# One shift term of the VectorE exponentials computed by GpSimd in four paired pieces, with the scheduler's constants retuned

## The chip, the cores and the metric

The kernel runs on one core of one Trainium2 chip. The metric is the device time of one execution in microseconds. A core has five engines that matter here: PE (TensorE, matrix multiply), DVE (VectorE), ACT (ScalarE), POOL (GpSimd) and SP (which issues DMAs). Each executes its own instructions in order; semaphores connect them. Times of a kernel agree within about 0.3% on a quiet chip. The granted TensorE clock differed between chips and runs in this study (0.97 to 1.00), and before's time with it (1559 to 1581 us), so it is given wherever it matters.

## The reference, cut to what matters

Four residual blocks in a row: A, B, A, B, on x of 2048 tokens x 512 features. A is attention with 32 query heads of size 16 and one shared key/value head; B is linear attention.

```python
def _A_ref(x, wq, wk, wv, wo):
    ...
    scores = jnp.einsum("bhqd,bkd->bhqk", q, k) * (Dh ** -0.5)
    p = _softmax(scores, axis=-1)
    o = jnp.einsum("bhqk,bkd->bhqd", p, v)
    ...
x = x + _A_ref(_layernorm(x, axis=-1), A_wq, A_wk, A_wv, A_wo)
x = x + _B_ref(_layernorm(x, axis=-1), B_wqkv, B_wo)
# ... and both once more
```

Block A dominates. Each of the two A layers has 2048 x 2048 x 32 scores. The kernel cuts them into 2048 blocks of 128 keys x 512 queries a layer, 4096 in all; each has to be computed (PE), exponentiated (ACT or DVE) and multiplied with the values (PE).

## The kernel before

The kernel contains a list scheduler. While the program is built, it simulates the five engines with fixed durations and a table of priorities and thresholds (the constants at its top), decides the order of instructions on each engine, and emits them in that order. Nothing is decided on the chip. In particular, which blocks go to ACT and which to DVE is settled at build time.

A block goes one of two ways.

ACT takes sets of three or two blocks from PSUM (banks 0 to 2, 3 to 4) in one exp instruction. Each block then needs one PV matmul.

```python
oe = add(AC, tac(m * 512), lambda e: e.activation(PTA[:, hp.idx, 0:m * 512], bank(SETS[s][0], m * 512), ACTF.Exp, scale=SCALE),
         deps=[o] + prevp, uses=[h, hp], rel=[h], prio=1.0, name="exp")
```

DVE takes single blocks from PSUM banks 5 and 6 and approximates exp by writing a scaled score as an integer whose bits are read as bf16 ("P1", one PSUM read a block). The approximation is refined by three more terms: copies of the tile with 32, 64 or 96 added to the integer ("xo", the shifts, 2048 columns for a batch of four blocks). PE adds the four terms up, with a scaled copy of the values for each. So a block on DVE needs four PV matmuls, and bank, DVE and PE in turn.

```python
o = add(PE, PASS, lambda e: self.smm(e, [p], db), ..., prio=0.01, name="sD", ...)          # score of one block
o = add(DV, tdv(512), lambda e: e.tensor_scalar(out=PTD[:, hp.idx, i * 512:(i + 1) * 512], in0=bank(db),
        scalar1=SCALE * LOG2E * 128.0, scalar2=TOFF, op0=ALU.mult, op1=ALU.add), ..., prio=PP1, name="P1")
...
def dpass(self, c):                                # a batch is full: its terms and PV matmuls
    ...
    for r in range(NTERM):                         # NTERM = 4
        dep, src = c["p1"], hp
        if r:
            dep, src = self.shift(c, m, r, done)
        for i, p in enumerate(c["pos"]):
            pv = self.add_pv(p, lambda src=src, i=i: PTD[:, src.idx, i * 512:(i + 1) * 512].bitcast(BF16), src, dep[0 if r else i], r, 1)
            ...
def shift(self, c, m, r, done):
    ...
        return e.tensor_scalar(out=PTD[:, ht.idx, 0:512 * m], in0=PTD[:, hp.idx, 0:512 * m], scalar1=float(SHIFT[r]), op0=ALU.add, **kw)
    o = add((DV, PO) if POOLX else DV, ..., prio=PX, cb=done, name="xo", port=True)
```

The softmax here doesn't subtract the row's maximum and nothing guards it: scores larger than these inputs give would overflow.

## Time and profile before

1562.74 us, median of 3 runs (1561.04 to 1565.96).

| before | value | view |
|---|---|---|
| PE, ACT, DVE, POOL busy | 96%, 95%, 94%, 11% | the page |
| ACT and DVE busy, 100-700 us | 97%, 96% | windows |
| blocks on ACT / on DVE | 3013 / 1083 | groups (PV and P1 counts) |
| 2048-wide shifts on DVE | 810, 0.67 us each | groups |

From the page: span, busy time by engine, granted PE clock in 40 slices, and the shares of the chain of waits that ended last.

```profile
span 1562.1 us, 41630 instructions
...
PE 1504.2 (96%) x18426; PEld 493.7 (32%) x18426; DVE 1467.4 (94%) x2631; ACT 1480.0 (95%) x1451; POOL 166.5 (11%) x225
...
PEclk9999999999999999999999999999999999999999
...
PE 58%; DVE 21%; ACT 20%; issue 1%; DMA 0%; POOL 0%; SPq 0%
...
```

PE, ACT and DVE are all nearly full; GpSimd is nearly idle (11%). The groups of DVE, ACT, POOL and PE that matter (columns: line, engine, operation, output<-input, shapes, count | busy us, mean ns | idle us just before them and what ended it):

```profile
...
L963 DVE TENSOR_SCALAR PTD<-ps_all 128x512 uint16<-128x512 f32 x1083 | 724.4, 682 | 42.8 <-PE ps_all L749 38.3
L1010 DVE TENSOR_SCALAR PTD<-PTD 128x2048 uint16<-128x2048 uint16 x810 | 546.3, 688 | 1.6
...
```

```profile
...
L906 ACT ACTIVATE PTA<-ps_all 128x1536 bf16<-128x1536 f32 (+1 forms) x1199 | 1386.6, 1282 | 40.6 <-PE ps_all L749 36.5
...
```

```profile
...
L1133 POOL TENSOR_TENSOR pqT<-e_buf 128x512 bf16<-128x512 f32 x28 | 38.4, 1376 | 10.2 <-DVE e_buf L1129 9.5
L1131 POOL TENSOR_SCALAR e_buf<-e_buf 128x512 f32<-128x512 f32 x56 | 37.9, 678 | 408.5 <-ACT e_buf L1122 408.4
...
```

```profile
...
L786 PE MATMUL ps_all<-PTD,Vaug 128*32 128x512 bf16 x4332 | 610.1, 386 | 13.3 <-DVE Eo L798 9.6 <-DVE PTD L1010 3.0
...
```

DVE waits little for its P1s (42.8 us), ACT little for its exps (40.6 us). GpSimd and the shifts disturb each other, as the timelines of DVE and POOL for the same moment show (columns: start us, us, instruction):

```profile
...
458.54 1.77 DVE L1010 TENSOR_SCALAR PTD<-PTD 128x2048 uint16<-128x2048 uint16 x1
460.23 0.24 DVE L811 RECIPROCAL rden<-ps_all 128x16 f32<-128x16 f32 x1
...
```

```profile
...
458.49 1.27 POOL L1133 TENSOR_TENSOR pk_tok<-e_buf 128x512 bf16<-128x512 f32 x1
```

The shift starts 0.05 us after GpSimd's add, and takes 1.77 us instead of 0.68. It ends 0.55 us after the add.

### The profile page before, as it was taken

What the parts mean: (1) busy time and instruction counts of PE and PEld (TensorE: products, weight loads), DVE (VectorE), ACT (ScalarE), POOL (GpSimd) and SP (SyncE); (2) the same over time, 40 slices, a digit from 0 to 9 for tenths busy, and PEclk for the clock granted to TensorE, in tenths of its full rate; (3) what the DMA queues carried; (4) which work ended last, traced back from release to release, by engine and by line L of the source; (5) the groups of instructions that cost most, each with busy time, mean ns of one, the idle gap of its engine ahead of it and who ended that gap; (6) DMA issues with size and microseconds to landing.
All of it is one profiled execution on the core that took longest, in us unless ns stands there. A gap on an engine that the chain in (4) does not pass through costs nothing.

```text
span 1562.1 us, 41630 instructions
## 1 busy us (share of the span) xinstructions
PE 1504.2 (96%) x18426; PEld 493.7 (32%) x18426; DVE 1467.4 (94%) x2631; ACT 1480.0 (95%) x1451; POOL 166.5 (11%) x225
## 2 busy tenths in 40 slices
PE   6999999999999999999899999999999999999998
PEld 4222222223323223332453222322223323223234
DVE  5999998999998999999799999999999999999987
ACT  6999999999999999999699999999999999999996
POOL 4000001002013001100330000000002112012011
PEclk9999999999999999999999999999999999999999
DMA  4000000000000000000000000000000000000001
GB/s 138 1 5 8 5 8 8 5 3 6 5 17 7 5 5 12 12 5 8 7 4 2 4 12 5 8 5 5 5 5 5 8 16 5 5 13 14 1 12 57
DMA packets 46181, 17.93 MB, mean 11 GB/s; under 512 B 39856, under 2 KB 45488, under 8 KB 46000
## 3 DMA queue, kind: packets, MB, share of 16 engines
q1 hardware_dynamic: 46000, 15.27, 4.1%
q8 instruction: 144, 2.36, 0.6%
q14 instruction: 37, 0.30, 0.1%
HBM read 5.28 MB, written 2.10 MB: 5 GB/s over the span
## 4 chain that ended last, share of the span: by engine, by line
PE 58%; DVE 21%; ACT 20%; issue 1%; DMA 0%; POOL 0%; SPq 0%
PE ps_all L786 23%; PE ps_all L749 23%; ACT PTA L906 18%; PE ps_all L498 10%; DVE PTD L963 10%; DVE PTD L1010 6%; PE ps_all L807 2%; DVE Eo L798 1%; ACT e_buf L1122 0%; DVE pqT L1252 0%; DVE x_sb L1114 0%; DVE stats L558 0%; PE ps_all L589 0%; ACT e_buf L1250 0%; DVE e_buf L1129 0%
## 5 line engine op out<-in xcount | busy, mean ns | idle before, releaser
L906 ACT ACTIVATE PTA<-ps_all 128x1536 bf16<-128x1536 f32 (+1 forms) x1199 | 1386.6, 1282 | 40.6 <-PE ps_all L749 36.5
L963 DVE TENSOR_SCALAR PTD<-ps_all 128x512 uint16<-128x512 f32 x1083 | 724.4, 682 | 42.8 <-PE ps_all L749 38.3
L749 PE MATMUL ps_all<-QT,Kr 32*128 32x512 bf16 x4154 | 679.1, 384 | 17.8 <-ACT PTA L906 12.8
L786 PE MATMUL ps_all<-PTD,Vaug 128*32 128x512 bf16 x4332 | 610.1, 386 | 13.3 <-DVE Eo L798 9.6
L1010 DVE TENSOR_SCALAR PTD<-PTD 128x2048 uint16<-128x2048 uint16 x816 | 547.9, 686 | 1.6
L786 PE MATMUL ps_all<-PTA,Vaug 128*32 128x512 bf16 x3013 | 532.8, 387 | 0.1
L749 PEld LDWEIGHTS ps_all<-QT,Kr 32*128 32x128 bf16 x4154 | 162.2, 91 | 502.6 <-ACT PTA L906 228.3
L786 PEld LDWEIGHTS ps_all<-PTD,Vaug 128*32 128x32 bf16 x4332 | 150.7, 94 | 218.1 <-issue 140.7
L786 PEld LDWEIGHTS ps_all<-PTA,Vaug 128*32 128x32 bf16 x3013 | 131.4, 94 | 187.5 <-issue 157.3
L566 POOL TENSOR_TENSOR rstd<-veps,mhalf 128x1 f32<-128x1 f32 x30 | 19.6, 654 | 875.5 <-DVE veps L564 875.5
L1131 POOL TENSOR_SCALAR e_buf<-e_buf 128x512 f32<-128x512 f32 x56 | 37.9, 678 | 408.5 <-ACT e_buf L1122 408.4
L498 PE MATMUL ps_all<-wqkv_sb,xnT 128*32 128x512 bf16 x1024 | 76.5, 388 | 0.6 <-DMA xnT<-xn_buf 0.4
L1122 ACT ACTIVATE e_buf<-ps_all 128x512 f32<-128x512 f32 x64 | 40.8, 641 | 12.6 <-PE ps_all L498 6.3
L498 PE MATMUL ps_all<-xnT,wq_sb 128*32 128x128 bf16 (+1 forms) x896 | 41.0, 293 | 4.1 <-issue 4.1
L558 DVE BATCH_NORM_STATS2 stats<-x_sb 128x6 f32<-128x512 bf16 x64 | 43.0, 678 | 0.8 <-DMA x_sb<-in_A_x_dram 0.7
L798 DVE COPY Eo<-ps_all 128x512 f32<-128x512 f32 x62 | 42.3, 682 | 1.0 <-PE ps_all L786 0.6
L1129 DVE TENSOR_SCALAR e_buf<-ps_all 128x512 f32<-128x512 f32 x56 | 38.1, 683 | 5.3 <-ACT e_buf L1122 5.0
L807 PE MATMUL ps_all<-identf,Eo 128*128 128x128 f32 x256 | 42.5, 289 | 0.2 <-DVE v_tok L1148 0.2
L498 PE MATMUL ps_all<-wo_sb,OT 128*32 128x512 bf16 x512 | 42.5, 382 | 0.0
L1133 POOL TENSOR_TENSOR pqT<-e_buf 128x512 bf16<-128x512 f32 x28 | 38.4, 1376 | 10.2 <-DVE e_buf L1129 9.5
L1133 POOL TENSOR_TENSOR pk_tok<-e_buf 128x512 bf16<-128x512 f32 x28 | 37.8, 1348 | 11.6 <-DVE e_buf L1129 8.7
L498 PE MATMUL ps_all<-xnT,wqkv_sb 128*32 128x128 bf16 (+1 forms) x896 | 37.4, 289 | 0.0
(90 smaller groups left out, 660.4 us busy)
## 6 DMA issues: line engine op xcount, KB each, us to landing
out_dram<-x_sb SPq DMA_DIRECT2D x16, 128.0 KB, 1.8
OT<-Osb SPq DMA_TRANSPOSE x120, 2.4
xnT<-xn_buf SPq DMA_TRANSPOSE x120, 2.4
wqkv_sb<-in_B_wqkv_dram SPq DMA_DIRECT2D x1, 1536.0 KB, 13.2
x_sb<-in_A_x_dram SPq DMA_DIRECT2D x3, 256.0 KB, 3.4
x_sb<-in_A_x_dram SPq DMA_DIRECT2D x1, 768.0 KB, 8.3
wq_sb<-in_A_wq_dram SPq DMA_DIRECT2D x1, 512.0 KB, 6.6
x_sb<-in_A_x_dram SPq DMA_DIRECT2D x1, 512.0 KB, 9.3
```

The costliest lines, as they stand in the source:

```text
L498: i = e.matmul(out[32 * c:32 * c + 32], lhsT=lhsT[:, 32 * c:32 * c + 32], rhs=rhs, start=start, stop=stop, skip_group_check=True)
L558: add(DV, tdv(512), lambda e: e.bn_stats(stats[:, t, 0:6], x_sb[:, t, :]), reads=[("x", t)], writes=[("st", t)], prio=prio, name="bn")
L749: x = e.matmul(bank(b0 + k), lhsT=Kr[r, m, kt * P:(kt + 1) * P], rhs=QT[r, self.units[u][0] % 2, gs, q0:q0 + n], start=True, stop=True)
L786: return e.matmul(ps[32 * c:32 * c + 32, 7 * 512:8 * 512], lhsT=Vaug[:, kt, r, :], rhs=src() if callable(src) else src, start=opened[0], s ...
L798: return (e.copy if oe.eng == AC else e.tensor_copy)(Eo[:, he.idx, :], bank(7))
L807: i = e.transpose(bank(ht.idx, P, qs * P), Eo[:, he.idx, qs * P:(qs + 1) * P], identf[:])
L906: oe = add(AC, tac(m * 512), lambda e: e.activation(PTA[:, hp.idx, 0:m * 512], bank(SETS[s][0], m * 512), ACTF.Exp, scale=SCALE), deps=[o] ...
L963: o = add(DV, tdv(512), lambda e: e.tensor_scalar(out=PTD[:, hp.idx, i * 512:(i + 1) * 512], in0=bank(db), scalar1=SCALE * LOG2E * 128.0, ...
L1010: return e.tensor_scalar(out=PTD[:, ht.idx, 0:512 * m], in0=PTD[:, hp.idx, 0:512 * m], scalar1=float(SHIFT[r]), op0=ALU.add, **kw)
L1122: o1 = add(AC, tac(512), lambda e: e.activation(e_buf[:, he.idx, :], bank(h.idx), ACTF.Exp), deps=[o], uses=[h], acq=[he] if fast else [he ...
L1129: o2 = add(DV, tdv(512), lambda e: e.tensor_scalar(out=e_buf[:, hr.idx, :], in0=bank(h.idx), scalar1=0.0, scalar2=1e-6, op0=ALU.max, op1=A ...
L1133: add(PO, PHS, lambda e: e.tensor_tensor(out=dst, in0=sh(e_buf[:, hr.idx, :]), in1=sh(e_buf[:, he.idx, :]), op=ALU.add), deps=[o2, o3], us ...
```

## The change

The intent: DVE is full and GpSimd idle, so GpSimd takes one of the three shifts of each full batch. A shift runs in a fast DVE mode that excludes GpSimd from SBUF, so the term is cut in four 512-wide pieces and each is tied to a DVE instruction that doesn't use the shared port: the scheduler starts a piece when DVE is in an instruction with at least PXM (0.55 us) left, and the piece then waits for the DVE instruction before that one. A piece that has waited PXA (4 us) may start in any DVE instruction that leaves the port free. Eleven older constants were retuned with it, most of all PX from 2.241 to 0.523 (shifts now come before P1s). The normalisation of odd tiles at a layer's start moved from GpSimd to DVE (PX1 = 0).

```diff
-HOLD = 0.75
+HOLD = 0.836
-PX = 2.241
+PX = 0.523
-PX1 = 1
-BK = 1.383
+PX1 = 0
+BK = 2.611
+NPX = 6
+PXP = 1.839
+PXM = 0.55
+PXA = 4.0
 ... (LEAD2, AF, EVP, PQP, PTR, BKX, PQL, PZ likewise)
@@ _try
+            if e == PO and o.pair and self.tfree[DV] - self.now < o.pair and self.now - o.rt < PXA - 1e-6:
+                self.at(o.rt + PXA, None)
+                continue
@@ _start
+        if e == PO and o.pair and len(self.order[DV]) > 1:
+            o.deps = o.deps + [self.order[DV][-2]]
@@ dpass
+                split = r == NTERM - 1 and m == 4 and self.npx < NPX and bool(p_ptd.free)
+                if split:
+                    dep, src = self.pieces(c, m, r, done)
+                elif r:
-                if r:
                     dep, src = self.shift(c, m, r, done)
@@ pieces (new; buffer bookkeeping cut)
+            for i in range(m):
+                def f(e, i=i):
+                    return e.tensor_scalar(out=PTD[:, ht.idx, i * 512:(i + 1) * 512], in0=PTD[:, hp.idx, i * 512:(i + 1) * 512], scalar1=float(SHIFT[r]), scalar2=1.0,
+                                           op0=ALU.add, op1=ALU.mult)
+                r_.append(add(PO, PXO[0] + 512 * PXO[1], f, deps=[c["p1"][i]] + prev, uses=[hp, ht], prio=PXP, cb=cb, name="xp", pair=PXM))
```

More of the change, by code (lines that the diff above doesn't have):

```diff
@@ L21 @@
 LX = 0.338
-HOLD = 0.75
+HOLD = 0.836
 LEAD = 16
-LEAD2 = 11
+LEAD2 = 14
 NT0 = 3
@@ L31 @@
 MF = 0.758
-AF = 2.752
+AF = 2.905
 PCONT = 0.992
-PX = 2.241
+PX = 0.523
 PP1 = 1.0
-EVP = 1.348
+EVP = 1.5
 EVX = 1.016
-PQP = 3.49
+PQP = 3.044
 PB = 1.6
@@ L41 @@
 PKV = 4.5
-PTR = 1.576
+PTR = 1.57
 PQF = 2
@@ L47 @@
 KC = 2
-PX1 = 1
-BK = 1.383
-BKX = 0.515
+PX1 = 0
+BK = 2.611
+BKX = 0.376
 BKR = 0.5
@@ L53 @@
 YD = 2
-PQL = 4.303
+PQL = 3.988
+NPX = 6
+PXP = 1.839
+PXM = 0.55
+PXA = 4.0
 PHL = 3.855
-PZ = 1.309
+PZ = 0.131
 SWITCH, PASS = 0.1, 0.217
@@ L62 @@
     __slots__ = ("engs", "fn", "dur", "prio", "deps", "nleft", "succ", "rt", "guard", "acq", "uses", "rel", "cb",
-                 "eng", "t0", "vis", "idx", "pk", "port", "kb", "gidx", "waits", "marked", "val", "vc", "dma", "done", "name")
+                 "eng", "t0", "vis", "idx", "pk", "port", "kb", "gidx", "waits", "marked", "val", "vc", "dma", "done", "name", "pair")
 class Holder:
@@ L109, in add @@
     def add(self, engs, dur, fn, reads=(), writes=(), prio=5.0, guard=None, acq=(), uses=(), rel=(), cb=None, deps=(),
-            dma=False, name="", pk=("F", ()), port=False, kb=0):
+            dma=False, name="", pk=("F", ()), port=False, kb=0, pair=0.0):
         o = Op()
-        o.pk, o.port, o.kb = pk, port, kb
+        o.pk, o.port, o.kb, o.pair = pk, port, kb, pair
         o.engs = engs if isinstance(engs, tuple) else (engs,)
@@ L695, in __init__ @@
             self.later = []
+            self.npx = 0
         def start(self, L):
@@ L993, in dpass @@
                 for i, p in enumerate(c["pos"]):
-                    pv = self.add_pv(p, lambda src=src, i=i: PTD[:, src.idx, i * 512:(i + 1) * 512].bitcast(BF16), src, dep[0 if r else i], r, 1)
+                    pv = self.add_pv(p, lambda src=src, i=i: PTD[:, src.idx, i * 512:(i + 1) * 512].bitcast(BF16), src, dep[0 if r and not split else i], r, 1)
                     def cb(o_, cb0=pv.cb, r=r, src=src, tc=tc):
@@ L1003, in dpass, with pieces, cb @@
                     pv.cb = cb
+        def pieces(self, c, m, r, done):
+            hp, ht = c["hp"], Holder(p_ptd)
+            ht.idx = p_ptd.free.pop(0)
+            prev = p_ptd.hist[ht.idx]
+            p_ptd.hist[ht.idx] = []
+            self.npx += m
+            n = {"n": 0}
+            def cb(o_):
+                self.npx -= 1
+                n["n"] += 1
+                if n["n"] == m:
+                    done(o_)
+            r_ = []
+            for i in range(m):
[3 more added lines that the diff above has]
+                r_.append(add(PO, PXO[0] + 512 * PXO[1], f, deps=[c["p1"][i]] + prev, uses=[hp, ht], prio=PXP, cb=cb, name="xp", pair=PXM))
+            return r_, ht
         def shift(self, c, m, r, done):
```

## The prediction

> **What bounds the kernel now.** The page of before gives PE 96%, DVE 94%, ACT 95% of 1562.1 us, POOL 11%. In the stretches 100-700 and 900-1450 us (windows view) ACT is busy 97-98%, DVE 96%. Most of it is attention: 4096 score blocks of 512 columns, each exponentiated by ACT (3013 blocks, 1386.6 us busy, 0.46 us each, line groups) or by DVE (1083). DVE pays for four blocks four PSUM reads (724.4 / 1083 = 0.67 us) and three 2048-wide SBUF shifts (0.67 us, 546 us in all): about 1.2 us a block. The static scheduler shares blocks so that both finish together; time falls only if blocks leave ACT. The chain of waits says PE 58%, DVE 21%, ACT 20%: but its 512-column passes, laid side by side by start, fill about 75% of the steady stretch: PE has some room, not much.
>
> **What the change does.** In full batches one of three DVE shifts becomes four 512-wide GpSimd pieces. A one-input 512-wide GpSimd op takes 0.61 us undisturbed (37 of the 56 min/max ops; mean of all 0.68). There are about 270 full batches; if all are split, DVE loses about 175 us of work and GpSimd gains about 1050 pieces, 650 us. The cap of six outstanding pieces and the need for a free buffer leave some unsplit: I guess 75-95% split. The rest is retuned priorities, and odd-tile normalisation moves from GpSimd to DVE (worth a microsecond or two).
>
> **Cost.** The page "SBUF — State Buffer" of the Trainium skill (Who interferes with whom) says GpSimd and a DVE op in a 2-port mode exclude each other for the whole instruction, and a one-input DVE op outside those modes doesn't contend. The trace agrees: a shift that starts during a GpSimd add ends 0.55 us after it, up to 1.77 us instead of 0.68; PSUM reads overlapped by GpSimd keep 0.68. But DVE steps every 0.60 us, and a piece starts about 0.08 us after the DVE end it waits for, itself 0.08 us into the next op, so it ends about 0.17 us after its partner. A shift next in line loses about 0.12 us. With 1000 pieces, half followed by a shift or delayed, I estimate 50-80 us of DVE time given back.
>
> **How much is on the critical path.** Let x be DVE's blocks. Before: 0.46(4096-x)+94 = 1.197x+171 gives x = 1090, near the 1083 seen. With one shift fewer everywhere 1.197 becomes 1.03: x = 1217, ACT 62 us less. With 85% split and 65 us lost to the port, net DVE relief is 85-100 us, of which 0.46/1.66 = 28% reaches the time: 24-28 us. More DVE blocks add three extra PV matmuls each.
>
> **Prediction.** 1537 us, range 1508 to 1562. Faster by over 2% 0.40, within 2% 0.53, slower 0.07.
>
> **What would show each step.** POOL busy 45-55%, 900-1080 new pieces at 0.61-0.70 us; 2048-wide shifts from 810 to 560-640; PSUM reads from 1083 to 1140-1200, ACT exp busy down 25-50 us; DVE still 93-96% busy; mean shift 0.70-0.80 us from port waits; PV matmuls on DVE blocks up 200-450. Wrong steps would show as DVE idle for PE, PE waiting for pieces, or shifts over 0.85 us.
>
> **What would make it wrong.** Faster: pairing so good that shifts keep 0.68 us (1510). Slower: the static order drifts on the chip, pieces start inside shifts, each collision costs up to 0.6 us and stalls the in-order PE; or PE, not ACT and DVE, is the true limit and absorbs the gain.

## More of the kernel before

Score matmuls use 32 rows of the PE array each, PV matmuls 32 columns each: two tiling modes, between which PE changes all the time.

A stretch of its timeline:

```profile
...
301.49 0.40 PE L786 MATMUL ps_all<-PTD,Vaug 128*32 128x512 bf16 x4
301.82 0.39 PE L749 MATMUL ps_all<-QT,Kr 32*128 32x512 bf16 x3
302.14 0.39 PE L786 MATMUL ps_all<-PTA,Vaug 128*32 128x512 bf16 x1
...
```

Three score matmuls (L749) start together at 301.82, and the first PV matmul (L786) after them at 302.14, 0.32 us later. Between passes of the same kind a pass starts 0.215 us after the last (starts of PV matmuls: up to four within 5 ns of each other, then 215 ns). The other 0.10 us belongs to the change of mode. It is remarkably constant: of 1103 changes between score and other matmuls in 100-700 us, the median extra time is 0.101 us one way and 0.099 the other. The Trainium skill, "TensorEngine Tiling (Array Packing)", Key Properties, says that a change of tiling mode drains TensorE; the trace agrees with a cost at each change and puts 0.10 us on it. In 100-700 us the columns streamed cover 454 us (matmuls laid side by side from their starts) and 1103 changes x 0.10 make 110: 564 of 600 us, 94%.

## The result, and the profile after

1552.05 us, median of 4 runs (1550.76 to 1553.27), against 1563.07 for before in the same rounds. The ratio is 0.9928, 95% interval 0.9910 to 0.9946: 0.7% faster where 1.65% was forecast. Ratios here are the mean time of one kernel's fast runs over that of the other's fast runs of the same rounds, so they are not quite the ratio of the medians quoted.

The page of after, then the groups that answer to those of before:

```profile
span 1549.8 us, 42215 instructions
...
PE 1489.3 (96%) x18337; PEld 499.5 (32%) x18340; DVE 1338.3 (86%) x2348; ACT 1479.1 (95%) x1458; POOL 807.5 (52%) x1297
...
PE 57%; ACT 33%; DVE 9%; issue 1%; DMA 0%; SPq 0%
...
```

```profile
...
L973 DVE TENSOR_SCALAR PTD<-ps_all 128x512 uint16<-128x512 f32 x1081 | 717.1, 684 | 133.6 <-PE ps_all L759 126.4
L1044 DVE TENSOR_SCALAR PTD<-PTD 128x2048 uint16<-128x2048 uint16 x540 | 359.2, 704 | 3.2 <-PE ps_all L796 0.3
...
```

```profile
...
L916 ACT ACTIVATE PTA<-ps_all 128x1536 bf16<-128x1536 f32 (+1 forms) x1202 | 1386.2, 1276 | 26.1 <-PE ps_all L759 22.3
...
```

```profile
...
L1034 POOL TENSOR_SCALAR PTD<-PTD 128x512 uint16<-128x512 uint16 x1080 | 655.1, 619 | 597.0 <-DVE PTD L1044 421.4 <-DVE PTD L973 97.1 <-DVE Osb L827 16.1
...
```

```profile
...
L796 PE MATMUL ps_all<-PTD,Vaug 128*32 128x512 bf16 x4324 | 624.8, 384 | 6.0 <-DVE Eo L808 3.0 <-DVE PTD L1044 2.2
...
```

The offload itself went as planned, better than forecast. All 270 full batches were split: 1080 pieces at 0.62 us, two 2048-wide shifts a batch left (540), DVE's busy time down by 129 us (1467.4 to 1338.3), GpSimd's up to 52%. The port cost next to nothing: summed over all shifts, the time beyond 0.69 us each is 10.9 us, against 6.4 before.

But the blocks did not move. DVE has 1081 P1s (1083 before), ACT's exps take 1386.2 us (1386.6), and the PV matmuls on DVE's tiles number 4324 (4332). DVE's freed time became idle time: its wait before P1s for scores from PE grew from 42.8 to 133.6 us. And yet 12 us were gained, nearly all of them out of ACT's idle time: 1562.1 - 1480.0 = 82.1 us before, 1549.8 - 1479.1 = 70.7 after.

How a piece sits beside its partner, on DVE and on POOL:

```profile
...
303.03 0.68 DVE L973 TENSOR_SCALAR PTD<-ps_all 128x512 uint16<-128x512 f32 x1
303.63 0.68 DVE L1163 TENSOR_SCALAR e_buf<-ps_all 128x512 f32<-128x512 f32 x1
...
```

```profile
...
303.19 0.62 POOL L1034 TENSOR_SCALAR PTD<-PTD 128x512 uint16<-128x512 uint16 x1 [1.92 <-DVE PTD L1044]
...
```

The P1 starts at 303.03, the piece 0.16 us later, and it ends 0.18 us into the next DVE instruction, where the prediction worked out 0.17. That one reads PSUM too, and doesn't mind.

### The profile page after: what moved, and what is told of

Read it like the earlier page. It is cut to its first block, busy times and chain, and to the rows that moved or that the text cites. A ratio compares the mean times of both kernels' runs of the same rounds, so it can differ in the third digit from the quotient of the medians.

```text
span 1549.8 us, 42215 instructions
## 1 busy us (share of the span) xinstructions
PE 1489.3 (96%) x18337; PEld 499.5 (32%) x18340; DVE 1338.3 (86%) x2348; ACT 1479.1 (95%) x1458; POOL 807.5 (52%) x1297
## 4 chain that ended last, share of the span: by engine, by line
PE 57%; ACT 33%; DVE 9%; issue 1%; DMA 0%; SPq 0%
ACT PTA L916 32%; PE ps_all L796 23%; PE ps_all L759 22%; PE ps_all L507 10%; DVE PTD L973 2%; DVE PTD L1044 2%; PE ps_all L817 2%; DVE stats L567 1%; DVE pqT L1286 1%; DVE e_buf L1163 1%; ACT e_buf L1156 1%; DVE xn_buf L586 0%; DVE Eo L808 0%; ACT e_buf L1284 0%; PE ps_all L598 0%
## 5 line engine op out<-in xcount | busy, mean ns | idle before, releaser
L916 ACT ACTIVATE PTA<-ps_all 128x1536 bf16<-128x1536 f32 (+1 forms) x1202 | 1386.2, 1276 | 26.1 <-PE ps_all L759 22.3
L1034 POOL TENSOR_SCALAR PTD<-PTD 128x512 uint16<-128x512 uint16 x1080 | 655.1, 619 | 597.0 <-DVE PTD L1044 421.4
L973 DVE TENSOR_SCALAR PTD<-ps_all 128x512 uint16<-128x512 f32 x1081 | 717.1, 684 | 133.6 <-PE ps_all L759 126.4
L759 PE MATMUL ps_all<-QT,Kr 32*128 32x512 bf16 x4187 | 658.9, 383 | 22.7 <-ACT PTA L916 15.8
L796 PE MATMUL ps_all<-PTD,Vaug 128*32 128x512 bf16 x4324 | 624.8, 384 | 6.0 <-DVE Eo L808 3.0
L1044 DVE TENSOR_SCALAR PTD<-PTD 128x2048 uint16<-128x2048 uint16 x543 | 359.8, 702 | 3.2 <-PE ps_all L796 0.3
L796 PEld LDWEIGHTS ps_all<-PTD,Vaug 128*32 128x32 bf16 x4324 | 160.3, 94 | 214.4 <-issue 129.1
L654 POOL TENSOR_SCALAR Vaug<-Vaug 128x32 bf16<-128x32 bf16 x48 | 15.4, 321 | 73.6 <-ACT Vaug L650 39.3
## 6 DMA issues: line engine op xcount, KB each, us to landing
wqkv_sb<-in_B_wqkv_dram SPq DMA_DIRECT2D x1, 1536.0 KB, 12.4
```

What stands on the lines that cost most here:

```text
L759: x = e.matmul(bank(b0 + k), lhsT=Kr[r, m, kt * P:(kt + 1) * P], rhs=QT[r, self.units[u][0] % 2, gs, q0:q0 + n], start=True, stop=True)
L796: return e.matmul(ps[32 * c:32 * c + 32, 7 * 512:8 * 512], lhsT=Vaug[:, kt, r, :], rhs=src() if callable(src) else src, start=opened[0], s ...
L1034: return e.tensor_scalar(out=PTD[:, ht.idx, i * 512:(i + 1) * 512], in0=PTD[:, hp.idx, i * 512:(i + 1) * 512], scalar1=float(SHIFT[r]), sc ...
```

## The experiments

Two theories at first. BALANCE is the prediction's: ACT and DVE bound the kernel and PE has room. PE: the TensorE loop (passes and mode changes) is full. Later a third came in: a tuned kernel is one draw of a greedy scheduler. Eighteen kernels ran, each beside before on the same chip. Times are medians, with the ratio to before; after's own ratio is 0.9928.

### One engine relieved at a fixed order

These kernels keep the order of all instructions and make some of one engine's narrower, so that stale columns are used and the result is wrong. First DVE (r == 2 is one of its shifts):

```diff
 def f(e):
+    n = 512 if r == 2 and ht.idx in SEEN else 512 * m     # full width at a buffer's first use
-    return e.tensor_scalar(out=PTD[:, ht.idx, 0:512 * m], in0=PTD[:, hp.idx, 0:512 * m], ...)
+    return e.tensor_scalar(out=PTD[:, ht.idx, 0:n], in0=PTD[:, hp.idx, 0:n], ...)
```

> Wrong result on purpose, same order of instructions as before. One of the three shifts of a full batch is made 512 instead of 2048 columns wide on VectorE (its other columns stay stale), so VectorE alone is relieved, by about 272 x 0.40 = 109 us, without GpSimd and without a new order. Theory BALANCE (ACT and DVE bound the kernel, PE has room, as the prediction had it): the time falls by some 20 us or more. Theory PE (the TensorE loop, passes plus 0.10 us at each change between score and PV matmuls, 96% of the steady stretch, is the limit): at most some 10 us fall, and VectorE shows the rest as idle time before the PSUM reads.

> Wrong result on purpose, same order as after. One of the two VectorE shifts that are left is made 512 wide: VectorE again relieved by about 109 us. Theory PE: 0 to 6 us off 1552, VectorE busy falls to some 79%. Theory BALANCE: 15 us or more off.

Then PE:

```diff
+rhs = src() if callable(src) else src
+n = 8 if r in (1, 2) and not opened[0] and not opened[1] else 512
-return e.matmul(ps[32 * c:32 * c + 32, 7 * 512:8 * 512], ..., rhs=src() if callable(src) else src, ...)
+return e.matmul(ps[32 * c:32 * c + 32, 7 * 512:7 * 512 + n], ..., rhs=rhs[:, 0:n], ...)
```

> Wrong result on purpose, same order as before. The PV matmuls of two of the four terms of VectorE's blocks are 8 instead of 512 columns wide (unless they open or close an accumulation): TensorE is relieved of about 530 passes of 0.21 us, less what a short matmul still takes, I estimate 60 to 100 us. Theory BALANCE: under 10 us off. Theory PE: 20 us or more off.

> Wrong result on purpose, same order as after, the same two terms 8 columns wide. Theory PE: more than the same cut gives before, 25 us or more off 1552. Theory BALANCE: under 10 us off.

And ACT:

```diff
-e.activation(PTA[:, hp.idx, 0:m * 512], bank(SETS[s][0], m * 512), ...)
+n = m * 512 - (256 if m == 3 and hp.idx in SEEN else 0)
+e.activation(PTA[:, hp.idx, 0:n], bank(SETS[s][0], n), ...)
```

> Wrong result on purpose, same order as before. Each 1536-wide exp on ScalarE is cut to 1280 columns (about 615 x 0.21 = 130 us less work for ACT; nothing else changes). Theory ACT (the time is ACT's work plus its idle time; ACT is 97-98% busy in the steady stretches, and relieving DVE or PE alone moved under 1%): 25 us or more off before. Theory NONE (no engine alone bounds a fixed order): under 10 us off, as DVE and PE did.

> Wrong result on purpose, same order as after, the same cut of 130 us on ACT. Theory ACT: more than before gains, since DVE now has slack: 40 us or more off 1552. Theory NONE: under 10 us off.

| relieved | order of before | order of after |
|---|---|---|
| DVE, busy -76 / -94 us | 1557.94 (0.9933) | 1549.03 (0.9856) |
| PE, columns and mode changes -63 / -62 us | 1578.26 (1.0024) | 1552.95 (0.9869) |
| ACT, busy -90 / -91 us | 1560.21 (0.9963) | 1533.94 (0.9809) |

The relief of PE is counted as above, over the whole span (1429 to 1366 us in before's order, 1412 to 1350 in after's). One of the four runs of fix_pe_after was slow (1577.93 us at clock 0.970): it is in the median and not in the ratio.

The runs of before which the DVE and PE rows are held against drifted from 1563 us at clock 0.996 to 1581 at 0.982, so those ratios look about half a per cent better than they are. Against after's 1552, relieving DVE by 94 us gains some 3 us, relieving PE nothing at the clocks that these runs had. BALANCE's picture of DVE as a limit fails: before gained about 5 us from 76 us of relief (its profiled run: 1557.5 at clock 0.996, before's 1562.1 at the same clock). No block can move at a fixed order, so this doesn't test the sharing of blocks on which the prediction rests. For PE alone the medians show no gain either, but they aren't a fair test. In the run of before's order the granted clock fell, and fix_pe_before was slower, not faster. The clock line of its page has dips that the page of before doesn't have:

```profile
...
PEclk9999999979999789999999699999999999999999
...
```

The Trainium skill, "TensorE: Matmul & The Clock Gate", Part 1, What's actually happening, says that activity is what releases the throttle. This run agrees in direction (mean granted clock 0.973, before's 0.996), so less PE work isn't a clean relief of PE. Nor is less PE work needed for a low clock: runs of before itself went down to 0.982. Compared at nearly the same clock, the order is the other way round: the one run of fix_pe_before at 0.984 took 1564.59 us, where before took 1579.53 at 0.983. That is 15 us off for 63 us less PE work, from a single run.

In before's order ACT's relief was hidden by the clock: two runs took 1550.60 and 1551.98 us at 0.996 and 0.994, two 1568.43 and 1569.34 at 0.983 and 0.981. At the high clock that is some 11 us off for 90 us of work, well short of the 25 expected. In the order of after, only ACT's relief showed clearly: 18 us for 90 us of work. It was less than expected (40 us), so something stands close behind ACT. The page of fix_act_after, busy times and chain:

```profile
...
PE 1481.2 (97%) x18340; PEld 490.8 (32%) x18340; DVE 1334.9 (87%) x2348; ACT 1388.0 (91%) x1458; POOL 806.6 (53%) x1297
...
PE 81%; DVE 15%; ACT 3%; issue 1%; DMA 0%; SPq 0%; POOL 0%
...
```

With ACT at 91%, PE makes up 81% of the chain. So relief in pairs was tried, combining the edits above:

> Wrong result on purpose, same order as after: the ScalarE cut of fix_act_after (90 us of ACT work, 18 us of time) and the PV cut of fix_pe_after (no time by itself) together. Theory PE NEXT (TensorE stands right behind ScalarE, so that relieving one alone hits the other): the two together give much more than 18 us, 1500 us or less. Theory LATENCY (fixed order, no engine's work matters, only the chain of waits): about 1530, as with ACT alone.

> Wrong result on purpose, same order as after: the ScalarE cut together with the VectorE cut of fix_dve_after (109 us of shifts). Theory PE NEXT: VectorE isn't the next limit, so 1524 to 1534, little beyond the 1534 of ACT alone. Theory DVE NEXT: 1515 or less.

Measured: ACT and PE 1515.47 (0.9673), ACT and DVE 1514.73 (0.9661). Both double the gain of ACT alone and neither is ahead. Neither expectation of the first run held (1500 or less, or about 1530), and the second met the mark set for DVE NEXT. So these runs don't rank PE and DVE. How relief of DVE helps once ACT is lighter isn't shown: PE's idle time put down to shifts was only 1.8 us in fix_act_after. What the fixed order does show is that no engine alone holds the time. The question of where the blocks went needs a new schedule.

### The two halves of the change alone

```diff
 # oldconst_pieces: after, with HOLD, LEAD2, AF, PX, EVP, PQP, PTR, PX1, BK, BKX, PQL, PZ as before had them
-PX = 0.523
+PX = 2.241
 ...
 # newconst_nopieces: after, with
-NPX = 6
+NPX = 0
```

> The code of after with every constant that before has set back to before's value: the GpSimd pieces alone. The program then gives VectorE 1129 blocks instead of 1081 and ScalarE 46 fewer (about 21 us less work). Theory BALANCE: the time falls below after's 1552, to about 1540. Theory PE CAP (TensorE can't feed both at that share): ACT's work falls by about 20 us but its idle time grows by as much or more, time 1550 to 1575.

> The code and constants of after with the cap of outstanding pieces at 0, so that no piece is made and VectorE does all three shifts: the retuned constants alone. VectorE takes 1000 blocks instead of 1083. If the gain of the change came from the constants alone: about 1552. If it came from the pieces: slower than before, 1570 to 1590, as ACT has 80 blocks or 37 us more to do.

| | before's constants | after's constants |
|---|---|---|
| no pieces | 1 (before), 1083 P1s | 1593.89 (1.0174), 1000 P1s |
| pieces | 1570.71 (1.0031), 1129 P1s | 1552.05 (0.9928), 1081 P1s |

The pieces alone, with before's constants, do move blocks: DVE gets 1129. The groups of P1 and of the exps in oldconst_pieces:

```profile
...
L973 DVE TENSOR_SCALAR PTD<-ps_all 128x512 uint16<-128x512 f32 x1129 | 755.0, 683 | 111.7 <-PE ps_all L759 101.8
...
```

```profile
...
L916 ACT ACTIVATE PTA<-ps_all 128x1536 bf16<-128x1536 f32 (+2 forms) x1181 | 1366.6, 1276 | 52.3 <-PE ps_all L759 48.1
...
```

ACT's exps fall by 20 us (1386.6 to 1366.6), as the balance of the prediction would have it, and its whole busy time by 17 us (1480.0 to 1462.7). Yet ACT's idle time rises from 82.1 to 1565.5 - 1462.7 = 102.8 us, more than was saved, and most of the growth before exps is a wait for PE's scores (48.1 us, before 36.5). PE CAP is met, BALANCE missed, as measured against the tuned before; the section on the draw of the constants weakens that. The constants alone lose 1.7% (a little more than the 1570 to 1590 us expected), with 1000 blocks on DVE:

```profile
...
L973 DVE TENSOR_SCALAR PTD<-ps_all 128x512 uint16<-128x512 f32 x1000 | 660.4, 683 | 112.6 <-PE ps_all L759 106.2
...
```

With them the pieces are worth 2.4% (0.9928 / 1.0174), move 81 blocks to DVE and take 37 us off ACT (1515.8 to 1479.1). So the pieces do move blocks at either set of constants, and the retuning takes about as many back: 83. Neither half gains alone against before.

### Lighter PV work, scheduled anew

If PE is what makes moved blocks unprofitable, then with less PV work the same move must pay. Two of the four PV terms of DVE's blocks are left out (their shifts are still made), before and in oldconst_pieces, and the scheduler runs anew:

```diff
 for r in range(NTERM):
     dep, src = c["p1"], hp
+    if r in (1, 2):
+        dep, src = self.shift(c, m, r, done)      # made, then given back unused
+        ...
+        continue
 ...
-    pv = self.add_pv(p, ..., r, 1)
+    pv = self.add_pv(p, ..., r, 3 if r == 0 else 1)
```

> Wrong result on purpose; before with two of the four PV terms of VectorE's blocks left out altogether, all three shifts still made, and the whole program scheduled anew for it. VectorE gets 1092 blocks. TensorE has about 540 passes or 115 us less. Theory PE CAP: without pieces VectorE is full as well (94%), so lighter PV work can't move blocks; the time falls little, to 1545 to 1560.

> Wrong result on purpose; the same two PV terms left out of oldconst_pieces, scheduled anew; VectorE gets 1121 blocks, as many as in oldconst_pieces (1129), which took 1571. Theory PE CAP: with TensorE lighter the same share of blocks pays: ScalarE's idle time falls back and the time is 1515 to 1530, so that pieces gain 30 us or more over pvcut_before instead of losing 5. Theory BANKS (the two PSUM banks or the rules of the scheduler hold VectorE back, not TensorE): 1550 or more.

Measured: pvcut_before 1573.82 (1.0050, interval 0.9999 to 1.0102), pvcut_oldconst_pieces 1540.17 (0.9803, interval 0.9740 to 0.9865). With full PV work on DVE's blocks the pieces lost 0.3% at before's constants; with half of it they gain 2.5% (0.9803 / 1.0050). DVE has 1121 P1s, so banks and rules let it take them, against theory BANKS. Two limits: each new order is a single draw of the scheduler (next section), and the edit gives the tiles of the unused shifts back at once, so the buffers of DVE's tiles are relieved along with PE. No run separates the two. ACT's exps in pvcut_oldconst_pieces:

```profile
...
L916 ACT ACTIVATE PTA<-ps_all 128x1536 bf16<-128x1536 f32 (+1 forms) x1187 | 1368.0, 1295 | 31.4 <-PE ps_all L759 28.4
...
```

They take 1368.0 us, as in oldconst_pieces, but the wait before them is 31.4 instead of 52.3 us, and ACT's idle time is 1536.0 - 1460.7 = 75.3 us. The time missed the expected 1515 to 1530: three of the four runs had a clock of 0.976 to 0.980, and the one at 0.992 took 1524.77. pvcut_before ran at 0.973 to 0.987, so its missing gain is partly the clock's.

### The draw of the constants

The scheduler is greedy, so a change of a priority by 1% gives another order. Each tuned constant was multiplied by a random factor between 0.99 and 1.01, in before, in oldconst_pieces and in after:

```diff
-HOLD = 0.75
-AP = 0.771
+HOLD = 0.7496
+AP = 0.7734
 ... (18 constants of before; jitter3 with another seed)
```

> before with each of its 18 tuned constants moved at random by at most 1%: VectorE 1084 blocks, hardly another share, another order. Theory DRAW (before is a tuned draw better than its neighbours): 1.0% slower than before, 1575 to 1590. Theory NO DRAW: within 0.4% of before.

> oldconst_pieces (pieces with before's constants) with the same constants moved at random by at most 1%: VectorE 1127 blocks. Theory DRAW: faster than jitter_before by 1% or more, 1555 to 1570, while oldconst_pieces against the tuned before showed nothing. Theory NO DRAW: as oldconst_pieces, no faster than jitter_before.

> after with the same kind of jitter, VectorE 1080 blocks. Theory DRAW: some 0.5% slower than after, 1555 to 1565, so 1.2% or more faster than jitter_before. Theory NO DRAW: within 0.4% of after's 1552.

> before with another random draw of at most 1% on each tuned constant; VectorE 1093 blocks. Theory DRAW: 0.7 to 1.8% slower than before. Theory CHANCE (the first pair was an accident): within 0.4% of before.

> after with a draw of the same kind and seed; VectorE 1078 blocks. Theory DRAW: slower than after by 0.3 to 0.9% and faster than jitter3_before by 1.0 to 2.0%. Theory CHANCE: faster than jitter3_before by under 0.8%.

| | time, us | ratio | clock of the runs |
|---|---|---|---|
| jitter_before | 1586.10 | 1.0117 | 0.984 to 0.987 |
| jitter_oldpieces | 1574.68 | 1.0036 | 0.986 to 0.992 |
| jitter_after | 1567.48 | 0.9986 | 0.989 to 0.996 |
| jitter3_before | 1598.05 | 1.0189 | 0.977 to 0.987 |
| jitter3_after | 1564.97 | 0.9972 | 0.989 to 0.995 |

All four neighbours of before and after are slower than the kernel they were drawn from (after's own ratio is from another chip): those of before by 1.2 and 1.9%, those of after by 0.6 and 0.4% (0.9986 and 0.9972 over 0.9928). Between neighbours the change gains 1.3% (0.9986 / 1.0117) and 2.1%, twice and three times what it gains between the tuned two. A part of that is the clock, which was lower in before's neighbours: the run of jitter3_before at 0.987 (1593.67) and that of jitter3_after at 0.989 (1569.46) are 24 us apart, the nearest runs of the first pair (1584.27 at 0.987, 1569.36 at 0.989) 15 us. Runs of before itself rose by 22 us from 0.998 to 0.982, 1.4 us for each 0.001, so some 3 us of either gap are the clock's: 0.8% and 1.4% remain. By that correction, the first pair shows hardly more than the tuned pair's 0.7%. Whether the lower clock is itself a result of the looser orders is open. With two draws each, the size of this effect is rough; that it exists in the uncorrected times is beyond their intervals.

jitter_oldpieces bears on oldconst_pieces. It is as fast as the kernel it was drawn from (1.0036 and 1.0031), and 0.8% faster than jitter_before (1.0036 / 1.0117), between its two theories; at the same clock of 0.986 it is 7 us faster (1577.59 and 1578.35 against 1584.94). So the pieces at before's constants lose 0.3% only against the tuned before; against a neighbour of before they gain. ACT's idle time also grows where no block has moved: to 1582.6 - 1480.4 = 102.2 us in jitter_before and 1600.4 - 1480.1 = 120.3 in jitter3_before. By the correction above some 13 and 21 us of that growth are the clock's (0.987 and 0.981 against 0.996). That leaves some 8 and 17 us for the draw, a good part of the 21 us by which oldconst_pieces idled more than before.

The exps of the first pair, jitter_before and then jitter_after:

```profile
...
L906 ACT ACTIVATE PTA<-ps_all 128x1536 bf16<-128x1536 f32 (+1 forms) x1200 | 1386.9, 1285 | 59.1 <-PE ps_all L749 55.5
...
```

```profile
...
L916 ACT ACTIVATE PTA<-ps_all 128x1536 bf16<-128x1536 f32 (+1 forms) x1203 | 1386.7, 1272 | 39.0 <-PE ps_all L759 34.8
...
```

And of jitter_oldpieces:

```profile
...
L916 ACT ACTIVATE PTA<-ps_all 128x1536 bf16<-128x1536 f32 (+1 forms) x1181 | 1369.0, 1270 | 53.4 <-PE ps_all L759 48.0
...
```

From jitter_before to jitter_after no ACT work went away (1386.9 and 1386.7 us): the gain is again ACT waiting less (59.1 to 39.0 us before its exps). In jitter_oldpieces 18 us of ACT work did go away, and ACT waited 53.4 us before its exps, no longer than in jitter_before.

### The pairing wait

```diff
-        if e == PO and o.pair and len(self.order[DV]) > 1:
-            o.deps = o.deps + [self.order[DV][-2]]
```

> after without the wait of each GpSimd piece for the VectorE instruction before the one that it is paired with (all other waits stay, the order is the same, the result correct). If the pairing wait protects the shared port: pieces start inside shifts, the time that shifts take beyond 0.69 us grows from 11 us to 40 us or more, and the time rises by some us. If the order alone keeps them apart: no change, within 0.3% of 1552.

Measured: 1606.58 us (1.0247), 3.2% slower than after (1.0247 / 0.9928), with a correct result and the same order of instructions. The shifts of after_nowait, and a collision on DVE and POOL:

```profile
...
L1042 DVE TENSOR_SCALAR PTD<-PTD 128x2048 uint16<-128x2048 uint16 x540 | 449.1, 870 | 3.0
...
```

```profile
...
296.29 0.68 DVE L971 TENSOR_SCALAR PTD<-ps_all 128x512 uint16<-128x512 f32 x1
297.00 1.90 DVE L1042 TENSOR_SCALAR PTD<-PTD 128x2048 uint16<-128x2048 uint16 x2
...
```

```profile
...
296.14 2.21 POOL L1032 TENSOR_SCALAR PTD<-PTD 128x512 uint16<-128x512 uint16 x3
```

Three pieces run back to back from 296.14, and the two shifts that start at 297.00 beside them take 1.90 us together, 0.95 each where an undisturbed one takes 0.68. Over all shifts the time beyond 0.69 us is 98.4 us instead of 10.9, and their mean 0.87 us instead of 0.70. PE's idle time before the PV matmuls on DVE's tiles grew from 6.0 to 20.7 us, and ACT's before its exps from 26.1 to 66.5. The wait, not the order, keeps the pieces off the shifts. The time went up by far more than the "some us" expected.

## Why the prediction was wrong

Right: ACT and DVE full, the number and duration of the pieces (1080 at 0.62 us; 900 to 1080 at 0.61 to 0.70 said), POOL at 52% (45 to 55), and the exclusion of GpSimd and shifts. That exclusion is what the Trainium skill, "SBUF — State Buffer", Who interferes with whom, states, and after_nowait shows it at full size. Time and range: 1552 lies in 1508 to 1562, and "within 2%" was the likeliest. That was luck in part: the 12 us came out of ACT's idle time and not, as forecast, out of its work. The forecast gain of 1.65% was more than twice the measured 0.7%.

**The step that failed** is "How much is on the critical path": "net DVE relief is 85-100 us, of which 0.46/1.66 = 28% reaches the time". The 28% assumed that freed DVE time is filled with blocks taken from ACT, and that "the rest is retuned priorities" leaves the shares alone. Predicted 1140 to 1200 P1s, 200 to 450 more PV matmuls and ACT's exps 25 to 50 us lighter; measured 1081, 8 fewer and 0.4 us. In its place came: DVE idle before P1s, from 42.8 to 133.6 us (named in the prediction as the sign of a wrong step), and ACT's idle time 11 us shorter at unchanged work.

**Why the blocks stayed.** The counts of P1s are fixed when the program is built, so they carry no noise. The pieces move 46 blocks to DVE at before's constants (1083 to 1129) and 81 at after's (1000 to 1081), as the step would have it; the retuning takes 83 away (1083 to 1000). Together that is 1081. This much is shown.

Why the retuned constants leave DVE with slack is argued and not shown. The candidate is PE. A block on DVE costs PE four PV matmuls instead of one, and a single score pass. The prediction saw PE "about 75%" filled and called that room, leaving out the mode changes: 0.10 us, 1.84 times a microsecond, which makes it 94%. For PE speaks that the pieces at before's constants are worth 2.5% with half the PV work on DVE's blocks (0.9803 against 1.0050), and with all of it -0.3% against the tuned before or 0.8% against its neighbour. Against taking this as proof stand the draws, which differ by about as much, and the tile buffers, which the same edit relieves. It is not that PE alone bounds the tuned orders: ACT with either PE or DVE gained about the same.

**The port cost was mis-sized.** 50 to 80 us of DVE time were to be given back; the shifts lost 4.5 us more than before (10.9 - 6.4). The overhang of 0.17 us was about right, but DVE has slack and the scheduler puts an instruction there that doesn't need the port. This error went the other way: had blocks moved freely, more would have been gained than predicted.

**The sign of the constants.** The prediction took the retuning for a detail. It is half of the change: against the tuned before, pieces without it lose 0.3%, it without pieces loses 1.7%. And both kernels are tuned draws, before a better one among its neighbours than after in the two pairs tried (uncorrected for the clock), so that the measured 0.7% is likely to understate the pieces. That part isn't settled.

**What stays open**: whether PE is what makes moved blocks pay less, by which of its costs (passes, mode changes, or their latency between bank and exp), and how much of the neighbours' loss is the clock. Open too is why ACT idles less in after. DVE's slack is one candidate. Another is in the traces: over the whole span PE changes between score and other matmuls 2492 times in after and 2640 in before (2590 in newconst_nopieces, 2624 in oldconst_pieces), which at 0.10 us each is 15 us less PE time. No run isolates it. No correct version that ran beat after.

## What to carry to other kernels

Relief of a full engine is worth only what the rest of the loop can use: when a change comes with retuned constants, count what each half does to the shares of work (here +81 and -83 blocks). Before converting freed time into moved work, add up the moved work's cost on every engine it passes, and for TensorE count changes of tiling mode beside the columns. When GpSimd works beside DVE's fast SBUF modes, tie its instructions to DVE instructions that leave the port free with a real wait; the order alone isn't enough (3.2% here). And compare a tuned kernel with a changed one over a few neighbours of each, or the luck of a draw of about 1% hides a change of the same size.

## What the Trainium skill lacked or had wrong

- "TensorEngine Tiling (Array Packing)", Key Properties, says that a change of tiling mode drains TensorE but not what it costs: 0.10 us here (medians 0.099 and 0.101 over 1103 changes), 110 of 600 us of the steady stretch.
- "Perfetto Trace Analysis", Identifying the Most-Contended Engine, takes LDWEIGHTS busy share (and MFU) for TensorE's measure. The LDWEIGHTS share is 32% here before and after, while columns and mode changes fill 94% of the steady stretch; the section counts no mode changes, so the LDWEIGHTS share alone would have shown much room on PE.
- "SBUF — State Buffer", Who interferes with whom, agrees with the runs. It doesn't say that a wait is needed to keep the two engines apart where order alone is planned: 98.4 us of excess shift time without the wait, 10.9 with it.
- "TensorE: Matmul & The Clock Gate", Part 1, ties the full clock to sustained activity, but says nothing of a PE that is recorded 95% busy and streams fewer columns. Granted clock here: 0.971 to 0.984 with two PV terms narrowed in before's order, 0.982 to 0.996 in before's runs of the same job. Whether the fewer columns caused it is not shown.
